# Linformer attention into a maxout FFN on one core: AV made transposed, sums by a ones matmul, q transposed by the DMA crossbar

## The chip, the core and the metric

The kernel runs on one core of a Trainium2 chip. Its engines work side by side, each through its own instructions in order: TensorE (PE, with its weight loads PEld), VectorE (DVE), ScalarE (ACT), GpSimd (POOL) and SyncE (SP). Sixteen DMA engines serve the queues of POOL and SP. The metric is the device time in microseconds; three runs of the kernel before give a median of 466.81 us.

## The reference

Eight batches of eight heads, 1024 positions of 64 elements. K and V are projected along the sequence from 1024 to 64 rows by E and F. Softmax attention over these 64 rows follows. The heads of a position, side by side (512 elements), go through a feed-forward network (FFN) with a maximum of three products.

```python
k_proj = np.einsum('ks,bhsd->bhkd', E, k)
v_proj = np.einsum('ks,bhsd->bhkd', F, v)
scores = scale * np.matmul(q, k_proj.transpose(0, 1, 3, 2))
attn = softmax(scores)                    # over the 64 projected rows
x = np.matmul(attn, v_proj)               # heads side by side: 8192 x 512
h = np.maximum(np.maximum(x @ w1, x @ w2), x @ w3)     # 768 wide
return h @ w_out                          # 8192 x 512, float32
```

## The kernel before

All inputs are cast to bf16 while GpSimd's queue loads them. The kernel is written in a framework whose scheduler fixes, when the program is built, the order of the instructions on each engine and puts in the waits; the order is therefore not just that of the source lines. Tiles come from pools with a number of buffers; an instruction that takes a buffer again waits until its earlier readers are done.

`attention(b)` handles one batch. It loads q, k and v in two halves of 0.5 MB each (L101; `work` has two buffers of each). The K projection `kp_ps` (L108: 16 matmuls of 256 columns, all into partitions 0 to 63) is evicted and transposed, and copied into the block-diagonal `kpT_bd`, two heads to a pair. For each of the four pairs g, a copy brings the pair's q into order (`q_p2`, L135, on VectorE, or on GpSimd for g of 2 and 3 from batch 1 on), eight TensorE transposes (L141) turn it, a copy brings it to SBUF (`qT_sb`, L147), two matmuls of 512 columns make the scores (L154), and ScalarE takes the exponent into `pT_g` (L160). The V projection (L172: 16 matmuls of 256 columns) fills `vp_bd`, which has a column of ones for each head (L189, L190), so that the AV matmul gives the sums as well.

Then for each of eight groups of 128 positions (si), four AV matmuls (L200) have positions on the partitions, VectorE takes the reciprocal of the sums (`zinv`, L209) and multiplies (`x_sb`, L210), four TensorE transposes (L220) turn the result, and a copy puts it into `xT` (L225).

`moe_chunk(b, xT, ch)` is the FFN over 512 positions, two chunks to a batch. For each of six blocks jt, 12 matmuls of 512 columns (L237) fill three banks of PSUM `h_ps`; ScalarE copies the first (`h1s`, L245), VectorE takes the two maxima (`m12`, L247, and `hT`, L248). Then 24 matmuls (L252) make four output tiles, which ScalarE copies to `o_acc` (L259), and SP's queue stores them (L261). The pool `ps_m` of the FFN has three banks, `ps_s` of attention five.

The loop runs attention of batch b ahead of the FFN of batch b-1; the scheduler weaves the two together. The weights (L85, L86) are loaded behind q, k and v of batch 0.

Of the kernel before, what the change touches and what calls it, by code (L numbers as in the profile page):

```python
# [8 lines left out]
FP32 = mybir.dt.float32  # L10
# [6 lines left out]
def kernel(  # L17
# [13 lines left out]
    nc = tc.nc  # L31
# [7 lines left out]
    P = 128  # L39
    SI = 8  # L40
# [10 lines left out]
    xt_pool = ctx.enter_context(tc.tile_pool(name="xt_pool", bufs=B))  # L51
    work = ctx.enter_context(tc.tile_pool(name="work", bufs=2))
    small = ctx.enter_context(tc.tile_pool(name="small", bufs=2))
    moe_sb = ctx.enter_context(tc.tile_pool(name="moe_sb", bufs=2))

    ps_s = ctx.enter_context(tc.tile_pool(name="ps_s", bufs=5, space=bass.MemoryType.PSUM))
    ps_m = ctx.enter_context(tc.tile_pool(name="ps_m", bufs=3, space=bass.MemoryType.PSUM))
# [7 lines left out]

    eT = const.tile([P, SI, KP], BF16, name="eT")
    fT = const.tile([P, SI, KP], BF16, name="fT")
    for src, dst in ((e_sb, eT), (f_sb, fT)):
        tp = ps_s.tile([P, 512], FP32, name="ps_s")
        tpb = tp.bitcast(BF16)  # L70
        src_v = src.rearrange("k (p si) -> k p si", si=SI)
        for si in range(SI):
            nc.tensor.transpose(
                out=tpb[:, si * KP:(si + 1) * KP],
                in_=src_v[:, :, si],
                identity=ident[:KP, :KP],
            )
        nc.any.tensor_copy(out=dst.rearrange("p si k -> p (si k)"), in_=tpb[:, :SI * KP])
# [9 lines left out]
    out_v = out.rearrange("(b p si) m -> b si p m", p=P, si=SI)  # L88

    def attention(b, pending):  # L90
        def drain(n=1):
            for _ in range(min(n, len(pending))):
                moe_chunk(*pending.pop(0))
        k_t = work.tile([P, H, SI, D], BF16, name="k_t")
        v_t = work.tile([P, H, SI, D], BF16, name="v_t")
        q_t = work.tile([P, H, SI, D], BF16, name="q_t")
        for src, dst in ((q[b], q_t), (k[b], k_t), (v[b], v_t)):
            sv = src.rearrange("h (p si) d -> p h si d", si=SI)
            for hh in range(2):
                hs = slice(hh * (H // 2), (hh + 1) * (H // 2))  # L100
                nc.gpsimd.dma_start(out=dst[:, hs], in_=sv[:, hs])  # L101


        kp_ps = ps_s.tile([P, 512], FP32, name="ps_s")
        for hh in range(2):
            hs = slice(hh * (H // 2), (hh + 1) * (H // 2))
            for si in range(SI):
                nc.tensor.matmul(  # L108
                    out=kp_ps[0:KP, hh * (H // 2) * D:(hh + 1) * (H // 2) * D],
                    lhsT=eT[:, si, :],  # L110
                    rhs=k_t[:, hs, si, :],
                    start=(hh == 0 and si == 0),
                    stop=(hh == 1 and si == SI - 1),
                )
        kp_sb = small.tile([P, H, D], BF16, name="kp_sb")
        nc.any.tensor_copy(out=kp_sb[0:KP], in_=kp_ps[0:KP].rearrange("a (h d) -> a h d", d=D))

        kpTs_ps = ps_s.tile([P, 512], FP32, name="ps_s").bitcast(BF16)
        for g in range(NPAIR):
            nc.tensor.transpose(  # L120
                out=kpTs_ps[:, g * KP:(g + 1) * KP],
                in_=kp_sb[0:KP, 2 * g:2 * g + 2, :],
                identity=ident[0:KP, 0:KP],
            )
        kpT_bd = small.tile([P, NPAIR, P], BF16, name="kpT_bd")
        nc.vector.memset(kpT_bd, 0.0)
        kpTs_v = kpTs_ps.rearrange("a (g x) -> a g x", x=KP)[:, :NPAIR, :]
        nc.any.tensor_copy(out=kpT_bd[0:D, :, 0:KP], in_=kpTs_v[0:D])  # L128
        nc.any.tensor_copy(out=kpT_bd[D:2 * D, :, KP:2 * KP], in_=kpTs_v[D:2 * D])

        pT = []
        for g in range(NPAIR):
            q_p2 = small.tile([P, SI, 2 * D], BF16, name="q_p2", bufs=3)
            peng = nc.vector if (b == 0 or g < 2) else nc.gpsimd
            peng.tensor_copy(  # L135
                out=q_p2.rearrange("p si (h d) -> p si h d", h=2),
                in_=q_t[:, 2 * g:2 * g + 2, :, :].rearrange("p h si d -> p si h d"),
            )
            qt_ps = ps_s.tile([P, 512], FP32, name="ps_s").bitcast(BF16)
            for si in range(SI):  # L140
                nc.tensor.transpose(  # L141
                    out=qt_ps[:, si * P:(si + 1) * P],
                    in_=q_p2[:, si, :],
                    identity=ident,
                )
            qT_sb = small.tile([P, SI, P], BF16, name="qT_sb", bufs=2)
            nc.any.tensor_copy(out=qT_sb, in_=qt_ps.rearrange("a (si p) -> a si p", p=P))  # L147

            pT_g = small.tile([P, SI, P], BF16, name="pT_g", bufs=5)
            pT.append(pT_g)  # L150
            for c in range(NCHUNK):
                sc_ps = ps_s.tile([P, 512], FP32, name="ps_s")
                csl = slice(c * SI_PER_CHUNK, (c + 1) * SI_PER_CHUNK)
                nc.tensor.matmul(  # L154
                    out=sc_ps,
                    lhsT=kpT_bd[:, g, :],
                    rhs=qT_sb[:, csl, :],
                    start=True, stop=True,
                )
                nc.scalar.activation(  # L160
                    out=pT_g[:, csl, :],
                    in_=sc_ps,
                    func=AF.Exp,
                    scale=scale,
                )

        vp_e = ps_s.tile([P, 512], FP32, name="ps_s")
        vp_o = ps_s.tile([P, 512], FP32, name="ps_s")
        for par, vt in ((0, vp_e), (1, vp_o)):
            rows = slice(0, KP) if par == 0 else slice(KP, 2 * KP)  # L170
            for si in range(SI):
                nc.tensor.matmul(  # L172
                    out=vt[rows, 0:NPAIR * D],
                    lhsT=fT[:, si, :],
                    rhs=v_t[:, par::2, si, :],
                    start=(si == 0),
                    stop=(si == SI - 1),
                )
        vp_bd = small.tile([P, NPAIR, 2 * (D + 1)], BF16, name="vp_bd")
        nc.vector.memset(vp_bd, 0.0)  # L180
        nc.any.tensor_copy(
            out=vp_bd[0:KP, :, 0:D],
            in_=vp_e[0:KP, 0:NPAIR * D].rearrange("a (g d) -> a g d", d=D),
        )
        nc.any.tensor_copy(  # L185
            out=vp_bd[KP:2 * KP, :, D + 1:2 * D + 1],
            in_=vp_o[KP:2 * KP, 0:NPAIR * D].rearrange("a (g d) -> a g d", d=D),
        )
        nc.vector.memset(vp_bd[0:KP, :, D:D + 1], 1.0)  # L189
        nc.vector.memset(vp_bd[KP:2 * KP, :, 2 * D + 1:2 * D + 2], 1.0)  # L190

        xT = xt_pool.tile([P, NCT, SI, P], BF16, name="xT")
        for si in range(SI):
            x_sb = small.tile([P, H, D], BF16, name="x_sb", bufs=3)
            for u in range(2):
                av_ps = ps_s.tile([P, 512], FP32, name="ps_s")
                av_v = av_ps.rearrange("p (g x) -> p g x", x=256)
                for gg in range(2):
                    g = 2 * u + gg
                    nc.tensor.matmul(  # L200
                        out=av_v[:, gg, 0:2 * D + 2],
                        lhsT=pT[g][:, si, :],
                        rhs=vp_bd[:, g, :],
                        start=(gg == 0),
                        stop=(gg == 1),
                    )
                av_b = av_v[:, :, 0:2 * (D + 1)].rearrange("p g (par y) -> p g par y", par=2)
                zinv = small.tile([P, 2, 2], FP32, name="zinv", bufs=3)
                nc.vector.reciprocal(out=zinv, in_=av_b[:, :, :, D:D + 1])  # L209
                nc.vector.tensor_tensor(  # L210
                    out=x_sb[:, 4 * u:4 * (u + 1), :].rearrange("p (g par) d -> p g par d", par=2),
                    in0=av_b[:, :, :, 0:D],
                    in1=zinv.broadcast_to([P, 2, 2, D]),
                    op=ALU.mult,
                )
            xt_ps = ps_s.tile([P, 512], FP32, name="ps_s").bitcast(BF16)
            xt_v = xt_ps.rearrange("p (ct x) -> p ct x", x=256)
            x_flat = x_sb.rearrange("p h d -> p (h d)")
            for ct in range(NCT):
# [84 lines left out]
```

The softmax here doesn't subtract the row's maximum and nothing guards it: scores larger than these inputs give would overflow.

## Time and profile before

| | |
|---|---|
| median of three runs | 466.81 us (466.43 to 467.7) |
| span of the profiled execution, first to last instruction | 465.2 us, 1.6 us under the median |
| TensorE busy | 431.2 us, 93% |
| VectorE busy | 228.9 us, 49% |
| ScalarE busy | 173.4 us, 37% |
| FFN matmuls on TensorE (L237, L252) | 263.8 and 85.1 us |
| read from and written to HBM | 57.15 and 16.78 MB |

The profile is of one execution. A line of a timeline has the start, the length, the engine, the line of the kernel, the operation, and the tile written and those read; in brackets the engine's idle time before it, and what ended it. The clock (PEclk) is the share of TensorE's full clock that was granted. Matmuls overlap each other, so the time of a run of them is read from its first start to its last end and not from the sum of their lengths. For DMAs, MB are counted at the destination.

### The profile page before, as it was taken

The page shows a single profiled execution, that of the slowest core. Times are in us where ns is not written, and L with a number is a line of the kernel's source. Part 1 is how long each engine was busy: PE and PEld are TensorE (multiplying, and loading weights), DVE is VectorE, ACT ScalarE, POOL GpSimd, SP SyncE. Part 2 cuts the span into 40 slices and gives each one's busy share as a digit, 9 for nine tenths or more (in the row PEclk, how much of TensorE's full clock was granted, in tenths as well). Part 3 has the DMA queues.
Part 4 walks back from the last instruction along what each step waited for, and adds up shares of the span by engine and source line. Part 5 has one row for each costly group of instructions (what it writes and reads, how often), then busy time and mean ns, then how long its engine had stood idle before and what let it go on. Part 6 is the DMA issues. An engine that isn't in the chain of part 4 may idle for free.

```text
span 465.2 us, 6667 instructions
## 1 busy us (share of the span) xinstructions
PE 431.2 (93%) x2623; PEld 226.4 (49%) x2672; DVE 228.9 (49%) x550; ACT 173.4 (37%) x311; POOL 54.7 (12%) x74
## 2 busy tenths in 40 slices
PE   1474999999999999999999999999999999999995
PEld 1343655455544555455544555455544555444442
DVE  2025575527934375426935376425935277334351
ACT  1142555235432543235532553235432453322322
POOL 7212240004000320005000320001000000000000
PEclk9996999999999999999999999999999999999999
DMA  8999999319620691209820592202020200202102
GB/s 118 207 210 206 208 205 207 111 80 171 113 92 0 144 201 20 92 41 189 133 92 1 132 193 39 92 0 92 2 91 0 92 1 0 92 0 92 56 36 90
DMA packets 30208, 45.78 MB, mean 98 GB/s; under 512 B 1121, under 2 KB 28001, under 8 KB 28129
## 3 DMA queue, kind: packets, MB, share of 16 engines
q0 software_dynamic: 27872, 28.58, 38.2%
q1 hardware_dynamic: 2304, 16.78, 8.7%
q8 instruction: 21, 0.34, 0.3%
q14 instruction: 11, 0.08, 0.1%
HBM read 57.15 MB, written 16.78 MB: 159 GB/s over the span
## 4 chain that ended last, share of the span: by engine, by line
PE 89%; DMA 8%; issue 1%; DVE 1%; POOL 1%; ACT 0%; POOLq 0%
PE ps_m L237 53%; PE ps_m L252 18%; DMA q_t<-in_q_dram 5%; PE ps_s L220 3%; PE ps_s L154 3%; PE ps_s L200 3%; PE ps_s L108 3%; PE ps_s L141 3%; DMA k_t<-in_k_dram 2%; PE ps_s L172 2%; PE ps_s L120 0%; DVE qT_sb L147 0%; POOL q_t L101 0%; DVE x_sb L210 0%; DVE zinv L209 0%
## 5 line engine op out<-in xcount | busy, mean ns | idle before, releaser
L237 PE MATMUL ps_m<-xT,w_sb 128*128 128x512 bf16 x1109 | 263.8, 380 | 2.5 <-issue 0.7
L237 PEld LDWEIGHTS <-w_sb 128*128 128x128 bf16 x1152 | 107.5, 98 | 111.8 <-issue 3.3
L245 ACT COPY h1s<-ps_m 128x512 f32<-128x512 f32 x96 | 56.3, 586 | 105.1 <-PE ps_m L237 104.2
L252 PE MATMUL ps_m<-wout_sb,hT 128*128 128x512 bf16 x378 | 85.1, 379 | 0.2
L259 ACT COPY o_acc<-ps_m 128x512 f32<-128x512 f32 x64 | 37.5, 585 | 71.4 <-PE ps_m L252 68.9
L252 PEld LDWEIGHTS <-hT 128*128 128x128 bf16 x384 | 37.3, 98 | 45.2 <-DVE hT L248 3.5
L225 ACT COPY xT<-ps_s 128x512 bf16<-128x512 bf16 x58 | 34.1, 587 | 60.3 <-PE ps_s L220 60.2
L210 DVE TENSOR_TENSOR x_sb<-ps_s,zinv 128x256 bf16<-128x256 f32 x128 | 48.6, 417 | 0.2
L160 ACT ACTIVATE pT_g<-ps_s 128x512 bf16<-128x512 f32 x64 | 34.8, 596 | 19.9 <-PE ps_s L154 19.9
L220 PE MATMUL ps_s<-ident,x_sb 128*128 128x128 bf16 x256 | 35.4, 226 | 5.7 <-DVE x_sb L210 5.6
L220 PEld LDWEIGHTS <-x_sb 128*128 128x128 bf16 x256 | 21.8, 100 | 24.9 <-DVE x_sb L210 13.2
L101 POOL DMA_DIRECT2D k_t<-in_k_dram x16 | 12.0, 753 | 166.1 <-PE ps_s L108 162.5
L200 PE MATMUL ps_s<-vp_bd,pT_g 128*128 128x130 bf16 x256 | 30.4, 227 | 0.5 <-DVE vp_bd L185 0.5
L147 DVE COPY qT_sb<-ps_s 128x1024 bf16<-128x1024 bf16 x31 | 21.4, 691 | 17.5 <-PE ps_s L141 17.5
L108 PE MATMUL ps_s<-k_t,eT 128*64 128x256 bf16 x128 | 17.5, 291 | 10.5 <-DMA k_t<-in_k_dram 10.2
L154 PE MATMUL ps_s<-qT_sb,kpT_bd 128*128 128x512 bf16 x64 | 20.9, 410 | 3.8 <-DVE qT_sb L147 2.4
L128 DVE COPY kpT_bd<-ps_s 64x256 bf16<-64x256 bf16 x6 | 1.7, 283 | 45.2 <-PE ps_s L120 45.2
L209 DVE RECIPROCAL zinv<-ps_s 128x4 f32<-128x4 f32 x128 | 17.8, 170 | 8.3 <-PE ps_s L200 8.1
L108 PEld LDWEIGHTS <-eT 128*64 128x64 bf16 x128 | 14.2, 116 | 13.8 <-issue 12.8
L200 PEld LDWEIGHTS <-pT_g 128*128 128x128 bf16 x256 | 19.5, 101 | 2.6 <-DVE vp_bd L185 2.6
L101 POOL DMA_DIRECT2D v_t<-in_v_dram x16 | 12.0, 762 | 14.2 <-PE ps_s L172 8.2
L172 PE MATMUL ps_s<-v_t,fT 128*64 128x256 bf16 x128 | 13.2, 291 | 0.0
(321 smaller groups left out, 259.0 us busy)
## 6 DMA issues: line engine op xcount, KB each, us to landing
out_dram<-o_acc SPq DMA_DIRECT2D x16, 1024.0 KB, 3.9
q_t<-in_q_dram POOLq DMA_DIRECT2D x16, 512.0 KB, 11.4
k_t<-in_k_dram POOLq DMA_DIRECT2D x16, 512.0 KB, 8.6
v_t<-in_v_dram POOLq DMA_DIRECT2D x16, 512.0 KB, 10.7
w_sb<-in_moe_w_dram POOLq DMA_DIRECT2D x3, 768.0 KB, 22.4
wout_sb<-in_moe_w_out_dram POOLq DMA_DIRECT2D x1, 768.0 KB, 24.9
e_sb<-in_E_dram POOLq DMA_DIRECT2D x1, 128.0 KB, 3.3
f_sb<-in_F_dram POOLq DMA_DIRECT2D x1, 128.0 KB, 3.2
```

What stands on the lines that cost most here:

```text
L101: nc.gpsimd.dma_start(out=dst[:, hs], in_=sv[:, hs])
L108: nc.tensor.matmul(out=kp_ps[0:KP, hh * (H // 2) * D:(hh + 1) * (H // 2) * D], lhsT=eT[:, si, :], rhs=k_t[:, hs, si, :], start=(hh == 0 an ...
L154: nc.tensor.matmul(out=sc_ps, lhsT=kpT_bd[:, g, :], rhs=qT_sb[:, csl, :], start=True, stop=True,)
L160: nc.scalar.activation(out=pT_g[:, csl, :], in_=sc_ps, func=AF.Exp, scale=scale,)
L200: nc.tensor.matmul(out=av_v[:, gg, 0:2 * D + 2], lhsT=pT[g][:, si, :], rhs=vp_bd[:, g, :], start=(gg == 0), stop=(gg == 1),)
L210: nc.vector.tensor_tensor(out=x_sb[:, 4 * u:4 * (u + 1), :].rearrange("p (g par) d -> p g par d", par=2), in0=av_b[:, :, :, 0:D], in1=zinv ...
L220: nc.tensor.transpose(out=xt_v[:, ct, 0:P], in_=x_flat[:, ct * P:(ct + 1) * P], identity=ident,)
L225: nc.any.tensor_copy(out=xT[:, :, si, :], in_=xt_v[:, :, 0:P])
L237: nc.tensor.matmul(out=h_ps[i], lhsT=w_sb[i][:, ct, jt * P:(jt + 1) * P], rhs=rhs_x[:, ct, :, :], start=(ct == 0), stop=(ct == NCT - 1),)
L245: nc.scalar.copy(out=h1s, in_=h_ps[0])
L252: nc.tensor.matmul(out=o_ps, lhsT=hT[:, jt, tt * P:(tt + 1) * P], rhs=wout_sb[:, jt, :], start=(jt == 0), stop=(jt == NJT - 1),)
L259: nc.scalar.copy(out=o_acc[:, tt, :], in_=o_ps)
```

## The change

The attention is written anew, and the order of the two halves of the work with it; the matmuls and evictions of the FFN stay.

- q: `q_p` is filled by four VectorE copies for all pairs of a batch (L117), and one DMA on SP's queue turns the whole of it by the DMA crossbar into `qT` (L122). The TensorE transposes of q and their evictions go.
- K: the projection's two halves of heads go to partitions 0 to 63 and 64 to 127 in turn (L130), so two transposes of 128x128 follow. V: eight matmuls of 512 columns (L155), with F twice beside itself in the weights.
- `kpT_bd` and `vp_bd` are constants with two buffers, set to zero once.
- AV: the weights are the block-diagonal `vp_bd`, the moving data `pT`, so the result has the head's elements on the partitions, as the FFN needs it. The output transposes and their evictions go. A second pair of matmuls with `ones_bd` gives the sums, spread over all 64 partitions of a head (L187).
- The sums are inverted on ScalarE as exp(-ln) in two passes of 128x1024 (L191, L193), and VectorE multiplies straight into `xT` (L194). ScalarE's table for both functions is loaded once at the start.
- `attention` and `ffn` are generators: one step of attention of batch b+1 after each step of the FFN of batch b; attention of batch 0 comes alone. Loads are whole (1 MB for each of q, k, v). Pools: `ps_f` three banks, `ps_a` two of two banks, `ps_p` one.

```diff
+        q_t, k_t, v_t = load(b)
+        q_p = att.tile([P, NPAIR, SI, 2, D], BF16, name="q_p")
+        for g in range(NPAIR):
+            nc.vector.tensor_copy(
+                out=q_p[:, g].rearrange("p si h d -> p h si d"),
+                in_=q_t[:, 2 * g:2 * g + 2, :, :],
+            )
+        qT = att.tile([P, NPAIR * SI, P], BF16, name="qT")
+        nc.sync.dma_start_transpose(
+            out=qT, in_=q_p.rearrange("p g si h d -> p (g si h d)")
+        )
+        yield
...
+        for si in range(SI):
+            for half in range(2):
                 nc.tensor.matmul(
+                    out=kp_ps[half * HALF:(half + 1) * HALF, 0:4 * D],
+                    lhsT=eT2[:, si, half, :],
+                    rhs=k_t[:, 4 * half:4 * half + 4, si, :],
+                    start=(si == 0), stop=(si == SI - 1),
                 )
...
-            qt_ps = ps_s.tile([P, 512], FP32, name="ps_s").bitcast(BF16)
-            for si in range(SI):
-                nc.tensor.transpose(
-                    out=qt_ps[:, si * P:(si + 1) * P],
-                    in_=q_p2[:, si, :],
-                    identity=ident,
-                )
...
+            sc = ps_a.tile([P, 2, 512], FP32, name="ps_a")
+            for c in range(2):
                 nc.tensor.matmul(
+                    out=sc[:, c, :],
                     lhsT=kpT_bd[:, g, :],
+                    rhs=qT[:, g * SI + 4 * c:g * SI + 4 * c + 4, :],
                     start=True, stop=True,
                 )
+            pT = att.tile([P, 2, 512], BF16, name="pT")
+            nc.scalar.activation(out=pT, in_=sc, func=AF.Exp, scale=scale)
+            yield
+            z = ps_a.tile([P, 2, 512], FP32, name="ps_a")
+            av = ps_a.tile([P, 2, 512], FP32, name="ps_a")
+            for dst, w in ((z, ones_bd), (av, vp_bd[:, g, :])):
+                for c in range(2):
                     nc.tensor.matmul(
+                        out=dst[:, c, :], lhsT=w, rhs=pT[:, c, :], start=True, stop=True,
                     )
-                nc.vector.reciprocal(out=zinv, in_=av_b[:, :, :, D:D + 1])
...
-            for ct in range(NCT):
-                nc.tensor.transpose(
-                    out=xt_v[:, ct, 0:P],
-                    in_=x_flat[:, ct * P:(ct + 1) * P],
-                    identity=ident,
-                )
+            zl = att.tile([P, 2, 512], FP32, name="zl")
+            nc.scalar.activation(out=zl, in_=z, func=AF.Ln)
+            zi = att.tile([P, 2, 512], FP32, name="zi")
+            nc.scalar.activation(out=zi, in_=zl, func=AF.Exp, scale=-1.0)
+            nc.vector.tensor_tensor(
+                out=xT[:, g].rearrange("a (c si) p -> a c (si p)", c=2),
+                in0=av, in1=zi, op=ALU.mult,
+            )
+            yield
...
+    for b in range(B):
+        main = ffn(b, box[b])
+        side = attention(b + 1, box) if b + 1 < B else iter(())
+        for _ in main:
+            next(side, None)
+        for _ in side:
+            pass
```

## The prediction

> **What bounds the kernel now.** I read the page's shares and slices first, then the chain that ended last, then the groups by form, and last the start of the run in detail. One batch of attention followed by one batch of the feed-forward network (FFN) is the unit; b is the batch, g the pair of heads.
>
> The page: busy shares, then TensorE, its clock and the DMA engines over 40 slices of 11.6 us.
>
> ```profile
> PE 431.2 (93%) x2623; PEld 226.4 (49%) x2672; DVE 228.9 (49%) x550; ACT 173.4 (37%) x311; POOL 54.7 (12%) x74
> PE   1474999999999999999999999999999999999995
> PEclk9996999999999999999999999999999999999999
> DMA  8999999319620691209820592202020200202102
> ```
>
> TensorE is full from slice 5 on; before that it waits, and the DMA engines are full for the first seven slices. The chain in order of time (start, length, what):
>
> ```profile
> 15.72 24.93 DMA q_t<-in_q_dram
> 101.09 1.86 PE ps_s L108 x16
> 418.34 4.96 PE ps_m L237 x23
> 455.73 4.06 PE ps_m L252 x18
> ```
>
> From the first matmul of batch 2 (101.0 us, L108) to the end of attention (418.3) lie six equal periods of 52.9 us with TensorE on the chain. The last FFN alone runs from 418.34 to 459.79: 192 matmuls in 41.45 us, 215.9 ns each. So attention costs 52.9 - 41.45 = 11.45 us of TensorE per batch, and from the last matmul to the end of the span pass 5.4 us (eviction, output DMA).
>
> Ahead of that, a line each of VectorE's and of TensorE's timeline (start, length, instruction, idle before it and what ended it):
>
> ```profile
> 40.67 0.43 DVE L135 COPY q_p_446<-q_t 128x1024 bf16<-128x1024 bf16 x1 [3.19 <-DMA q_t<-in_q_dram]
> ```
> ```profile
> 41.71 0.40 PE L220 MATMUL ps_s<-ident,x_sb 128*128 128x128 bf16 x2 [3.72 <-DVE x_sb L210]
> ```
>
> This is the pattern my forecast turns on: a q copy for batch 1 stands in VectorE's order ahead of batch 0's x_sb, the copy waits for its load, and TensorE idles 3.72 us. The granted clock then stood at 0.50 from 37.6 to 47.8 us.
>
> DMA queues in two windows, 79 to 81 us and 81.9 to 82.9 us:
>
> ```profile
> q0 software_dynamic: 419, 0.41, 124.7%
> ```
> ```profile
> q0 software_dynamic: 115, 0.11, 65.7%
> q1 hardware_dynamic: 26, 0.21, 51.7%
> ```
>
> Alone, loads move 0.205 MB per us (packets of 1 KB), back to back from 5 to 84 us: a 0.5 MB half lands every 2.54 us. The moment an output DMA runs beside them they fall to 0.11. The load engines have no free room.
>
> **The change, TensorE.** Steady terms first. Removed per batch: 32 q transposes (8 took 0.62 us warm), 32 output transposes (L220), 32 AV matmuls of 130 columns (L200; a pair of both groups runs in 0.23 to 0.43 us). Kept: 8 score matmuls. Added: 8 sum matmuls with ones_bd and 8 AV matmuls, each 512 columns. V's projection becomes 8 of 512 columns instead of 16 of 256. So 32 x 0.216 = 6.92 us, two kp transposes 0.15, and K's projection: 16 of 256 columns took 1.86 us here, all in one half of the partitions; now two halves alternate, 0.93 if a pair overlaps fully. I take 1.4. Attention becomes 8.45 us (8.0 to 8.95), a saving of 3.0 us per batch, some 20 us over seven batches if TensorE never waits.
>
> **Evictions.** ScalarE per batch: three passes of 128x1024 per g. The ScalarE copy of that size took 1.012 us, so 12 x 1.02 = 12.2, plus 20 FFN copies at 0.586, plus two vp copies at 0.37: about 24.7 of a 50 us period. VectorE: 24 maxima at 0.692, four products of 1024 at 1.23 (417 ns at 256, 692 at 512, extended), four copies at 0.42: 24 us. Both fit. Locally: after z and AV, Ln and Exp hold ScalarE until 2.74 us, h1s until 3.37, the product holds VectorE to 4.07 and the next maximum ends at 4.8, where TensorE wants its bank at 4.76. With hand-offs of 0.1 to 0.2 us that is some 0.1 us lost per g, 28 times; I take 2 us, bounds 0 to 14 (half a microsecond each).
>
> **The start, where it is decided.** The loads keep their order and bytes: q, k, v of b=0, weights, then q, k, v of b=1, 2, 3, 4. Batch 1's first q half lands at 40.65 (15.72 + 24.93). To the end of q of b=4 come 19 more halves: 40.65 + 19 x 2.54 = 88.9 us. That each load is now one DMA of 1 MB changes no byte. On GpSimd's queue k and v of b=3 stand ahead of q of b=4 and wait for the projections of batch 1, done by some 57 and 72 us, before the loads ahead of them have drained: nothing.
>
> What moves: in the changed program all four q copies of batch b (L117) go ahead of the crossbar transpose (L122), and VectorE's order has them early. Those of b=1 stand before the last product of b=0; of b=2 before the third maximum of FFN(0); of b=3 before the sixth; of b=4 before the first maximum of FFN(0)'s second chunk. Behind each stand all later maxima, so h_ps is not evicted and TensorE stops after three banks. In the kernel before, b=2 was copied at 56 us just as it landed and later ones far behind, at no cost. Now the second chunk of FFN(0) can't pass until q of b=4 has landed.
>
> By then TensorE has done chunk 0 of FFN(0) and 16 matmuls of chunk 1, and attention(1) up to g=1. That is some 36 us of work available from about 50 us (q of b=1 gates the last product of b=0), so even with its earlier stops it arrives first; this also hides the first transpose's own latency, up to some 30 us. Left after the stop: 1424 FFN matmuls x 0.2159 = 307.4, g=2 and 3 of attention(1) 2.6, six attentions 50.7: 360.7 us.
>
> **The crossbar's price.** Eight transposes of 1 MB, SBUF to SBUF, on SP's queue, on the same 16 engines. The trace has none. Lower bound: an output DMA of 1 MB in 8 KB packets, 8.7% of the span over 16 transfers, 2.5 us each; less is excluded since the engines were full. Upper bound: 32 blocks x 128 partitions are 4096 pieces of 256 B; at a 1 KB packet's price (1024 in 5.08 us) 20 us. I take 5.1, the row with the same megabyte in middling pieces. Transposes of b=0, 1, 2 come before q of b=4 and delay it by 15.2 us. On SP's queue the first output follows them, and transpose 3 follows that output; both start about 97 us and halve the loads for the last 6.4 us, so 6.4 more. q of b=4 lands at 88.9 + 15.2 + 6.4 = 110.5 us.
>
> The Trainium skill, page "VectorE: DVE Perf Modes", section "The three transpose paths", speaks against this change: 1309 ns for a 128x128 block by the crossbar against 390 ns on TensorE, where this trace has 8 TensorE transposes in 0.62 us. As an estimate by that page 32 blocks are 41.9 us, and if all of it were engine time the sum would be near 600. The page "DMA: Bandwidth & Descriptors", section "Latency and other measured facts", gives 261 GB/s for a DMA transpose, by which one is an estimated 4.0 us and the sum 482. No run here shows either yet.
>
> **Sum.** Landing 110.5; four copies, a maximum and hand-offs 2.6; remaining TensorE work 360.7; tail 5.4; evictions 2; clock 3 (the one drop seen lasted 10.2 us at half, partly in the idle time; 0 to 5). Span 484.2 against 465.2. The median of the runs is 1.6 above the span, so 485.8, put as 486.
>
> **Rivals.**
> The crossbar is cheap and TensorE's saving shows: loads are hardly delayed, q of b=4 lands at 90, K's halves overlap (six times 0.45 less), no clock drop or stalls: 90 + 2.6 + 358 + 5.4 + 1.6 = 457.6, faster. For it: TensorE is the chain for 90% of the span and loses 3 us a batch. Against: full engines until 84 us. It decides when q of b=4 lands before 95 us, that is a transpose of under 1 to 2 us.
> The crossbar is dear: at 20 us the landing is 88.9 + 61 + 6.4 = 156 and the time 532; at 10 us 501. For it: small pieces. Against: nothing in the trace but the volume.
> Eviction stalls: half a microsecond at each of 28 places adds 12, 498. Against: 65% busy shares.
> Ln and Exp could reload tables (1.28 us, seen once), but the built order has one load, so this is left out.
>
> **How the numbers follow.** Forecast 0.53 (472 to 495, crossbar 2.5 to 7 us), dear crossbar 0.22, eviction stalls 0.08, cheap crossbar 0.17, of which 0.04 within 0.3% of before. 0.3% (1.4 us) is about what a measurement of this kernel tells from no change. So faster 0.13, same 0.04, slower 0.83. The range leaves out the cheap case and the dear one beyond 20 us: 468 to 530.
>
> **What would show it.** Right: q copies on VectorE waiting for q_t loads between 60 and 115 us, TensorE idle in slices 5 to 9, the clock at 0.5 there, a period near 50 us from batch 2 on, an unchanged tail. Step by step: the landing of q of b=4 (110), the duration of a transpose's packets (5.1), attention per batch (8.45). Wrong: TensorE full from 50 us on, or periods above 53 us, or TensorE waiting for qT in later batches.

## The result and the profile after

The changed kernel takes 484.65 us (median of four, 483.62 to 485.96) against 466.95 for the kernel before on the same chip: a ratio of 1.0371, interval 1.0347 to 1.0396. It is slower by 17.7 us; the forecast was 486. The profiled execution's span is 483.7 us. One execution of a later run, the plain copy, took 2445 us; it is left out as disturbed.

The page of the changed kernel, TensorE, its clock and the DMA engines in 40 slices of 12.1 us:

```profile
PE   0200768087999999999999999999999999999995
PEclk9999999579999999999999999999999999999999
DMA  8999999999969433862467146616202020202012
```

TensorE now idles in slices 3 and 4 (24 to 48 us) and again in slice 8 (85 to 97 us), where the clock has fallen to half. From slice 11 on it is full. The chain of the changed kernel in order of time (start, length, what):

```profile
14.02 35.19 DMA qT<-q_p
...
66.72 48.38 DMA qT<-q_p x2
...
143.14 0.99 PE ps_p L130 x16
...
436.85 15.54 PE ps_f L208 x72
...
473.11 5.19 PE ps_f L225 x24
```

So 35.2 + 48.4 us of the first 115 are crossbar transposes (48.4 is transposes 1 and 2 together); no load of q is on this chain. The q copies of batches 1, 3 and 4 on VectorE, and then the stops on TensorE (start, length, instruction, idle before it and what ended it):

```profile
65.26 1.43 DVE L117 COPY q_p<-q_t 128x1024 bf16<-128x1024 bf16 x4
98.73 1.53 DVE L117 COPY q_p<-q_t 128x1024 bf16<-128x1024 bf16 x4 [14.90 <-DMA qT<-q_p]
115.19 1.43 DVE L117 COPY q_p<-q_t 128x1024 bf16<-128x1024 bf16 x4 [7.42 <-DMA qT<-q_p]
```
```profile
49.25 1.01 PE L174 MATMUL ps_a<-qT,kpT_bd_93 128*128 128x512 bf16 x2 [29.03 <-DMA qT<-q_p]
98.68 1.01 PE L174 MATMUL ps_a<-qT,kpT_bd_94 128*128 128x512 bf16 x2 [15.58 <-DMA qT<-q_p]
117.28 1.89 PE L208 MATMUL ps_f<-xT,w_sb 128*128 128x512 bf16 x8 [2.56 <-DVE m_489 L218]
```

TensorE's two long stops, 29.0 and 15.6 us, are its own waits for `qT` of batches 0 and 1: the scores stand next in its order. On VectorE the copies of batch 3 wait for transpose 1 and those of batch 4 for transpose 2, because `q_p` has two buffers; the FFN's maxima stand behind them. Only the second of these waits shows on TensorE by itself, as the 2.56 us before 117.28. The load of batch 4's q had landed at 103.7 us already.

Why a transpose is so long shows in the queues of the changed kernel, first from 20 to 48 us (beside the loads), then from 126.5 to 133 us (alone): packets, MB, share of the 16 engines. For the second the rate in 40 slices stands first, the time from issue to landing last.

```profile
q0 software_dynamic: 3770, 4.56, 92.7%
q1 hardware_dynamic: 3772, 0.97, 26.2%
```
```profile
GB/s 13 13 13 0 17 183 224 219 216 210 206 216 224 213 221 210 216 221 225 216 222 214 219 214 216 219 216 216 217 219 216 216 214 186 238 27 0 0 0 0
...
q1 hardware_dynamic: 4128, 1.05, 86.0%
...
qT<-q_p SPq DMA_TRANSPOSE x1, 7.3
```

The transpose goes in some 4100 packets of 256 B, and beside the loads one of them passes for each load packet of 1 or 1.5 KB: 3772 against 3770. From issue to landing it takes 7.3 us alone and 35 in company. The loads fall from 0.205 MB per us (the kernel before) to 0.163.

One period of the steady part in the changed kernel (stretch, its length, busy times of TensorE, its weight loads, VectorE, ScalarE, GpSimd, then clock and DMA):

```profile
143.07:192.90 49.83, 49.83 (x245) 22.72 (x246) 23.38 (x36) 23.79 (x34) 1.75 (x2) 1.00 0.60 134
```

It is 49.83 us, all TensorE, against 52.9 before. Six periods bring back 18.4 us of a start that lost about 37: FFN(0) and attention(1) were done at 101.1 us before, at 138.0 now.

### The profile page after: what moved, and what is told of

Read it like the earlier page. It is cut to its first block, busy times and chain, and to the rows that moved or that the text cites. A ratio compares the mean times of both kernels' runs of the same rounds, so it can differ in the third digit from the quotient of the medians.

```text
span 483.7 us, 4961 instructions
## 1 busy us (share of the span) xinstructions
PE 407.9 (84%) x1952; PEld 184.0 (38%) x1952; DVE 191.2 (40%) x291; ACT 192.9 (40%) x273; POOL 26.3 (5%) x36
## 4 chain that ended last, share of the span: by engine, by line
PE 74%; DMA 21%; ACT 2%; DVE 1%; POOL 0%; issue 0%; POOLq 0%; DVEq 0%
PE ps_f L208 47%; DMA qT<-q_p 19%; PE ps_f L225 16%; PE ps_a L187 5%; PE ps_p L155 3%; PE ps_a L174 3%; DMA k_t<-in_k_dram 2%; PE ps_p L130 1%; ACT zl L191 1%; ACT zi L193 1%; ACT pT L181 1%; DVE q_p L117 0%; POOL q_t L107 0%; DVE hT L219 0%; PE ps_p L141 0%
## 5 line engine op out<-in xcount | busy, mean ns | idle before, releaser
L208 PE MATMUL ps_f<-xT,w_sb 128*128 128x512 bf16 x1152 | 263.9, 381 | 4.4 <-DVE m_489 L218 2.6
L225 PE MATMUL ps_f<-wout_sb,hT 128*128 128x512 bf16 x384 | 87.3, 379 | 0.4 <-DVE hT L219 0.4
L216 ACT COPY h1s<-ps_f 128x512 f32<-128x512 f32 x96 | 55.8, 581 | 74.7 <-PE ps_f L208 73.8
L194 DVE TENSOR_TENSOR xT<-ps_a,zi 128x1024 bf16<-128x1024 f32 x32 | 39.2, 1225 | 92.4 <-ACT zi L193 55.1
L181 ACT ACTIVATE pT<-ps_a 128x1024 bf16<-128x1024 f32 x32 | 32.8, 1024 | 90.3 <-PE ps_a L174 90.3
L232 ACT COPY o_acc<-ps_f 128x512 f32<-128x512 f32 x64 | 37.1, 584 | 51.6 <-PE ps_f L225 51.3
L191 ACT ACTIVATE zl<-ps_a 128x1024 f32<-128x1024 f32 x32 | 32.8, 1024 | 45.2 <-PE ps_a L187 45.1
L174 PE MATMUL ps_a<-qT,kpT_bd_93 128*128 128x512 bf16 x32 | 9.9, 393 | 29.6 <-DMA qT<-q_p 29.0
L193 ACT ACTIVATE zi<-zl 128x1024 f32<-128x1024 f32 x32 | 33.8, 1057 | 1.0
L117 DVE COPY q_p<-q_t 128x1024 bf16<-128x1024 bf16 x32 | 12.3, 432 | 32.6 <-DMA qT<-q_p 22.7
L174 PE MATMUL ps_a<-qT,kpT_bd_94 128*128 128x512 bf16 x32 | 9.9, 393 | 15.6 <-DMA qT<-q_p 15.6
L187 PE MATMUL ps_a<-pT,ones_bd 128*128 128x512 bf16 x64 | 19.5, 387 | 4.0 <-ACT pT L181 4.0
L155 PE MATMUL ps_p<-v_t,fT_102 128*128 128x512 bf16 x64 | 16.8, 410 | 0.0
L130 PE MATMUL ps_p<-k_t,eT_101 128*64 128x256 bf16 x128 | 9.9, 294 | 1.9 <-DMA k_t<-in_k_dram 1.9
L187 PEld LDWEIGHTS <-ones_bd 128*128 128x128 bf16 x64 | 6.3, 99 | 12.4 <-issue 5.4
```

The costliest lines, as they stand in the source:

```text
L155: nc.tensor.matmul(out=vp_ps, lhsT=fT2[:, si].rearrange("p x k -> p (x k)"), rhs=v_t[:, :, si, :], start=(si == 0), stop=(si == SI - 1),)
L174: nc.tensor.matmul(out=sc[:, c, :], lhsT=kpT_bd[:, g, :], rhs=qT[:, g * SI + 4 * c:g * SI + 4 * c + 4, :], start=True, stop=True,)
L181: nc.scalar.activation(out=pT, in_=sc, func=AF.Exp, scale=scale)
L187: nc.tensor.matmul(out=dst[:, c, :], lhsT=w, rhs=pT[:, c, :], start=True, stop=True,)
L191: nc.scalar.activation(out=zl, in_=z, func=AF.Ln)
L193: nc.scalar.activation(out=zi, in_=zl, func=AF.Exp, scale=-1.0)
```

## The experiments

Theory A: in the start a transpose is long because its small packets take turns with the loads' packets, and the order on TensorE and VectorE passes that length on to the FFN; in the steady part the change gains 3 us a batch. Theory B: the loads and their extra megabytes are the gate. Theory C: the rest of the rewrite costs it. Each ratio is to the kernel before on the same chip; the landmark for the start is the first K projection of batch 2 (L130 in the changed kernel; some edits shift the line number), at 143.1 us in the changed kernel.

**A plain copy in place of the transpose.**

```diff
-        nc.sync.dma_start_transpose(
-            out=qT, in_=q_p.rearrange("p g si h d -> p (g si h d)")
+        nc.sync.dma_start(
+            out=qT, in_=q_p.rearrange("p g si h d -> p (g si) (h d)")
         )
```

> The crossbar transpose (L122) is replaced by a plain copy of the same megabyte, SBUF to SBUF, on the same queue, with the same waits and the same instruction order; so the scores are made of q that is not transposed. Theory A, the packets: in the changed kernel a transpose goes in 4096 packets of 256 B, one beside each load packet of 1 KB, so it takes 35 us beside the loads (7 us alone) and holds up everything behind it in VectorE's and TensorE's order. A plain copy in large packets takes 3 to 6 us: qT of batch 0 at about 20 us, the FFN of batch 0 from about 48 us, the last stop at the landing of batch 4's q, 88.9 + 4 x 2.5 = 99 us; then 2.1 + 361 + 5.4: a span of 467, time 464 to 472. Rival B, the megabyte: the extra volume and the landing of batch 4's q are the gate, whatever the packets: within 1% of the changed kernel, 480 or more. Rival C, the rest of the rewrite (two extra passes on ScalarE, the new order): also 480 or more.

> The plain copy in place of the transpose once more, for its trace: the scores are made of q that is not transposed. Theory A: a copy lands in 3 to 6 us beside the loads, loads keep over 0.15 MB per us, the copies of batch 4 on VectorE wait for their load and not for a DMA of SP's queue, until about 100 us; period 49.8.

472.1 us, ratio 1.0102 (1.0075 to 1.0128): 0.1 us over what theory A gave, and well under the 480 of both rivals. The trace is of a further execution of the same kernel (473.02 us). From 18 to 22 us, and VectorE's last copies in the start:

```profile
q1 hardware_dynamic: 134, 1.02, 62.7%
q0 software_dynamic: 286, 0.29, 46.8%
```
```profile
99.97 1.43 DVE L117 COPY q_p<-q_t 128x1024 bf16<-128x1024 bf16 x4 [13.89 <-DMA q_t<-in_q_dram]
```

The same megabyte in 8 KB packets passes in some 4 us and the loads give way to it, to 0.07 MB per us. From issue to landing the three copies beside the loads take 9.5, 7.5 and 7.6 us, more than the 3 to 6 expected. Now the copies of batch 4 wait for their load, until 100 us, and L130 of batch 2 comes at 130.2. So the crossbar costs 12.5 us against a plain copy of the same bytes. That the size of its packets does it rests on the count, 3772 against 3770; no run changes the size alone. What is left over the kernel before, 1%, theory A puts down to VectorE's order with the loads; the next four runs bear on that.

**TensorE transposes again, all else as changed.**

```diff
-        nc.sync.dma_start_transpose(...)
+        for g in range(NPAIR):
+            qt_ps = ps_p.tile([P, 512], FP32, name="ps_p").bitcast(BF16)
+            for si in range(SI):
+                nc.tensor.transpose(out=qt_ps[:, si * P:(si + 1) * P], ...)
+            nc.vector.tensor_copy(out=qT[:, g * SI:(g + 1) * SI, :], ...)
```

> q is transposed on TensorE again (32 transposes and four evictions of 128x1024 on VectorE per batch) in one step ahead of the K projection; no crossbar; all else as changed. Theory A: the start is no longer held by transposes, the FFN of batch 0 starts at about 48 us; the period rises from 49.8 by 4 x 0.62 to 52.3 us. 48 + 8 x 41.45 + 7 x 10.9 + 5.4 = 461, with some waits for loads 461 to 468. Rival C (the rewrite's order, not the crossbar, costs the start): 478 or more.

471.84 us, ratio 1.0095 (1.0072 to 1.0118): 3.8 us over the upper end expected. The period is 51.8 us, 2.0 more than with the crossbar, so the crossbar's worth in the steady part is 12 us over six periods. Without it the start still stops for q's loads, as the copies of b=2 and 3 stand ahead of maxima here too (start, length, idle before it and what ended it):

```profile
58.48 0.43 DVE L117 COPY q_p<-q_t 128x1024 bf16<-128x1024 bf16 x1 [4.61 <-DMA q_t<-in_q_dram]
...
73.71 0.43 DVE L117 COPY q_p<-q_t 128x1024 bf16<-128x1024 bf16 x1 [8.04 <-DMA q_t<-in_q_dram]
```

The expected time had left these stops and the clock's drops (three between 45 and 80 us) out. The crossbar therefore is not the whole loss, and theory C's part is this order.

**Four buffers for q_p.**

```diff
-        q_p = att.tile([P, NPAIR, SI, 2, D], BF16, name="q_p")
+        q_p = att.tile([P, NPAIR, SI, 2, D], BF16, name="q_p", bufs=4)
```

> q_p gets four buffers instead of two; nothing else. In the changed kernel the copies of batch 3 wait 14.9 us for transpose 1 to give back its buffer, those of batch 4 wait 7.4 us for transpose 2. Theory A (the transpose's own length is the gate): TensorE needs qT of batch 1 at 98.7 us anyway, so only the second wait's share goes, about 3 us: 480 to 483. Rival D (the buffers are the gate): both waits go, 15 to 20 us, 464 to 470.

491.31 us, ratio 1.051 (1.0486 to 1.0535): slower than either theory said. The copies of batch 3 no longer wait for a buffer (they run at 85.6 us), but TensorE still waits for qT of batch 1:

```profile
99.18 1.01 PE L174 MATMUL ps_a<-qT,kpT_bd 128*128 128x512 bf16 x2 [14.26 <-DMA qT<-q_p]
```

And with buffers free the scheduler put the copies of batches 5 and 6 still further ahead, among the maxima of FFN(0)'s second chunk, where those of batch 6 wait for their load:

```profile
125.10 1.10 DVE L117 COPY q_p<-q_t 128x1024 bf16<-128x1024 bf16 x3 [5.77 <-DMA q_t<-in_q_dram]
```

L130 of batch 2 comes at 148.3, 5.2 us later. A wait for a buffer had also been holding the copies back.

**The copies of batches 1 to 7 on GpSimd.**

```diff
-            nc.vector.tensor_copy(
+            (nc.vector if b == 0 else nc.gpsimd).tensor_copy(
```

> The q copies of batches 1 to 7 go from VectorE to GpSimd (about 1.04 us each there); the crossbar stays. Theory A: transpose 1 can start when its q has landed and been copied, 49.4 + 4.2 = 54 us instead of 66.7, and is done at about 87 instead of 98.7; VectorE holds up no maximum any more, so TensorE stops once, until 87, and then never: 12 us from that, 3 to 4 us from the later stop and the clock: 466 to 472. Rival B (loads or total DMA volume are the gate): within 1% of the changed kernel.

467.69 us, ratio 1.0006 (0.9993 to 1.0019), as theory A had it. The copies wait on GpSimd, up to 31 us, and nothing of the FFN stands behind them:

```profile
POOL q_p L117 <- DMA qT<-q_p: 87.2, 4, 30.7
POOL q_p L117 <- DMA q_t<-in_q_dram: 46.5, 3, 31.0
```

Transpose 1 in the chain (start, length):

```profile
53.25 31.93 DMA qT<-q_p
```

It lands at 85.2 us instead of 98.6, TensorE passes its scores at 85.2 with no stop, and L130 of batch 2 comes at 124.5, 18.6 us earlier. Most of this, 13.5 us, is the earlier start of transpose 1: in the changed kernel the copies of batch 1 stood behind three products of batch 0 on VectorE, until 65.3 us, though their q had landed at 49.4. The stop that the copies of batch 4 made gives 2.6 more. So the place of the q copies in VectorE's order is worth about as much as the whole loss; the crossbar's company with the loads decides how long the rest must wait for them.

**One transpose per pair.**

```diff
+        for g in range(NPAIR):
+            nc.sync.dma_start_transpose(
+                out=qT[:, g * SI:(g + 1) * SI, :],
+                in_=q_p[:, g].rearrange("p si h d -> p (si h d)"),
+            )
```

> One crossbar transpose per pair of heads (256 KB) instead of one per batch; VectorE's order as changed. Theory A (packets share one for one, the length goes by their number): the quarters of batch 0 land at about 23, 32, 41 and 49 us, its attention runs beside them, the copies of batch 1 come at about 53 instead of 65 us, transposes 1 and 2 end some 8 to 12 us earlier: 472 to 478. Rival E (a transpose has a large fixed cost each): no gain or a loss, 484 or more.

484.73 us, ratio 1.0379 (1.0356 to 1.0402): no gain, though the quarters of batch 0 landed at 25.4, 34.6, 42.2 and 49.0 us and transpose 1 was complete at 83.0. Transpose 2 then shared the engines with the loads in its turn, until 110.9, 28 us:

```profile
111.07 1.43 DVE L117 COPY q_p<-q_t 128x1024 bf16<-128x1024 bf16 x4 [17.18 <-DMA qT<-q_p]
```
```profile
113.16 3.57 PE L210 MATMUL ps_f<-xT,w_sb 128*128 128x512 bf16 x8 [9.38 <-DVE m L220]
```

TensorE resumes 4.1 us earlier, but at a granted clock of 0.50 until 117.2 us (eight matmuls 3.57 us against 1.89 in the changed kernel), and the first K projection of batch 2 comes 2.1 us earlier, at 141.0. The time is what rival E had named (484 or more) and not theory A's 472 to 478. But E's cause, a large fixed cost of each transpose, is not seen: the four quarters of batch 0 took 36.2 us together, one transpose 35.2. What counts is where the last transpose of the start ends, and theory A's number had missed that.

**A reciprocal on VectorE for Ln and Exp.**

```diff
-            nc.scalar.activation(out=zl, in_=z, func=AF.Ln)
-            nc.scalar.activation(out=zi, in_=zl, func=AF.Exp, scale=-1.0)
+            nc.vector.reciprocal(out=zi, in_=z)
```

> Ln and Exp on ScalarE are replaced by one reciprocal of 128x1024 on VectorE. Theory A: evictions are hidden in the period (49.8 us against 49.45 of TensorE's own work); at the start each pair is 0.9 us shorter, so the copies of batch 1 and what follows come about 2.5 us earlier: 480 to 485. Rival C (the two passes on ScalarE bind): the period falls too, 475 to 479.

570.19 us, ratio 1.2203 (1.2172 to 1.2235): both expectations fail, for the price of the reciprocal. The group in this kernel, and the two passes in the changed one:

```profile
L191 DVE RECIPROCAL zi<-ps_a 128x1024 f32<-128x1024 f32 x32 | 209.6, 6551 | 40.0 <-PE ps_a L187 39.6
```
```profile
L191 ACT ACTIVATE zl<-ps_a 128x1024 f32<-128x1024 f32 x32 | 32.8, 1024 | 45.2 <-PE ps_a L187 45.1
L193 ACT ACTIVATE zi<-zl 128x1024 f32<-128x1024 f32 x32 | 33.8, 1057 | 1.0
```

One reciprocal takes 6.55 us, exp(-ln) 2.08. With the sums spread over 64 partitions there are 1024 numbers per partition to invert instead of four at a time, and of the two ways run here the table passes are the cheaper by a factor of three. Whether ScalarE binds the period this run can't tell, as VectorE became the bound.

**Both remedies: GpSimd copies, TensorE transposes for batches 0 and 1.**

```diff
-            nc.vector.tensor_copy(
+            (nc.vector if b == 0 else nc.gpsimd).tensor_copy(
...
+        if b < 2:
+            (the four groups of TensorE transposes and copies as above)
+        else:
             nc.sync.dma_start_transpose(...)
```

> Two things together: the q copies of batches 1 to 7 on GpSimd, and q of batches 0 and 1 transposed on TensorE, so that the crossbar runs only from batch 2 on, whose result is not needed before about 105 us. Theory A (in the start a transpose beside the loads takes 35 us and TensorE waits for it; later it is hidden, and the period is 49.8): scores of batch 0 from about 24 us, FFN from 46 to 48, FFN(0) and attention(1) done at about 101 instead of 119 us with the GpSimd copies alone, all else the same: 447 to 454, faster than both kernels. Rival B (the loads and their total volume are the gate): 460 or more.

446.98 us (445.51 to 448.49), ratio 0.957 (0.9545 to 0.9595): 4.3% faster than the kernel before, at the lower edge of what was expected. The start of the kernel with both, 50 to 100 us in the columns of the period shown above:

```profile
50.00:100.00 50.00, 49.96 (x249) 22.90 (x248) 23.36 (x34) 23.89 (x34) 12.29 (x14) 1.00 1.25 199
```

TensorE is full from 50 us while the DMA engines move 199 GB/s, as they do in the changed kernel from 30 to 45 us (198), no drop of the clock shows before the last matmul, and L130 of batch 2 comes at 103.0, 40 us earlier than in the changed kernel. The period stays 49.8. FFN(0) and attention(1) are done at 97.8 us, against 101.1 before. So the loads were not the bound, with crossbar transposes beside them too.

## Why the prediction was right, and where it was not

- **The steady part: right.** Attention at 8.45 us a batch was the term; measured 49.83 - 41.45 = 8.38. K's projection with alternating halves took 0.99 us (taken: 1.4; lower end 0.93), so the alternation overlaps nearly wholly. TensorE's own work then is 8.0, and 0.4 a batch is left, which I put down to evictions (not shown one by one): 2.4 us over six batches for the 2 taken. The tail is 5.4 as before.
- **VectorE's order as the place of the loss: right in part.** The last stop fell where the text had it: resume at 117.28, last matmul at 478.3, 361.0 us between them where 360.7 + 2 stood. But the copies ahead of the maxima cost TensorE only the 2.56 us before it. The long stops, 29.0 and 15.6 us, were TensorE's own waits for qT, and without the wait of b=3 on VectorE (four buffers) the second still lasted 14.3. The costlier place in VectorE's order was another: the copies of b=1, late behind the products.
- **What the copies wait for: wrong.** The step "q of b=4 lands at 110.5 us" named the load; it landed at 103.7. The stop ended with transpose 2, at 115.1. The step that failed is the one before it, "this also hides the first transpose's own latency, up to some 30 us": transposes 0 and 1 took 35.2 and 32 us beside the loads, one after the other, TensorE stood 29.0 and 15.6 us for them, and the buffers of `q_p` chained the copies to them. Of the signs named, the copies' waits for q_t loads between 60 and 115 us did not show. The plain copy shows the forecast's version: there the load does end the stop, at 99.97.
- **The crossbar's price: near as engine time, missing as a wait.** Taken 5.1 us of the engines; alone its packets take 5.6 (86.0% of 6.5 us), beside the loads some 8 (26.2% of 28 us for 0.97 MB). That prices the load's delay well: ahead of q of b=4 came two transposes and the beginning of a third and not three and an output, so it was delayed 14.8 us and not 21.6. But copies and scores wait for the landing, and from issue to landing a transpose takes 7.3 us alone and 32 to 35 beside the loads; for this the sum has no term. The load was 6.8 us earlier than forecast, the gate that took over 4.6 us later, and the 3 us for the clock were not lost. That the total is off by 1.4 us is partly luck.
- **The clock: 3 us taken, none lost.** The drop (85.8 to 102.9 us) fell into the time before the last stop.
- **The rules weighed.** Of the Trainium skill, the 261 GB/s of the page "DMA: Bandwidth & Descriptors", section "Latency and other measured facts", (an estimated 4.0 us; the page gives it for a non-contiguous middle dimension) is not met here: while a transpose alone moves, the trace shows some 216 GB/s, and from issue to landing 1.05 MB in 7.3 us are 144. The 1309 ns a block of its page "VectorE: DVE Perf Modes", section "The three transpose paths", is nearer to what a block costs beside the loads (35.2 / 32 = 1.10 us) than to what it costs alone (0.23). A rule that would have helped stands in the first of these pages, section "Queues, rings and completion order": an engine takes queues in turn, packet by packet. The trace agrees as far as it counts packets, 3772 against 3770 (whether its packets are those of the page no run here shows). By that rule 4096 packets let as many load packets pass, an estimated 4 x 5.08 = 20 us from the load row, and with the 5.6 us of its own packets some 26. Measured from issue to landing are 35.2 and 32 us, and 28 for transpose 2 of the split kernel. The estimate leaves out the 4 us before the first transpose's packets move (two from 14 to 18 us) and that some of its neighbours have 1.5 KB.
- **Rivals.** A cheap crossbar did not come. The dear one came in another form: as latency, not as engine time, and it cost 12.5 us (against the plain copy) and not 46. Eviction stalls of 12 us did not come.

## What to carry to other kernels

Price a DMA that shares engines by its number of packets against its neighbour's, not by its bytes: here small packets beside a saturated load queue stretched it from 7.3 to 35 us, and what waits is its consumer and whatever stands behind that in an engine's order. Look up that order in the built program: a copy that a scheduler has put early, in free buffers, becomes a stop for everything after it when its data come late, and more buffers can make it worse; one that stands late delays the DMA that it feeds. Put such copies on an engine that nothing urgent uses, and keep the slow path for what is not needed soon: in the kernel with both remedies the transposes of batches 2 and 3 still took 32.7 and 28.4 us, and TensorE did not wait.

## What the runs showed of the hardware that I had not expected

- One crossbar transpose of 1 MB, from issue to landing: 7.3 us alone, 35.2 and 32 us for the first two, beside the loads.
- A reciprocal of 128x1024 floats out of PSUM takes 6551 ns on VectorE; the product of the same size, with the same source, 1225.
- Two runs of matmuls with 64 output partitions each, alternating between the halves: 16 of 256 columns in 0.99 us, against 1.86 when all go to one half.
- TensorE's granted clock stood at half for part of the start in every trace but the one with both remedies, from 6.8 us in all (GpSimd copies) to 47 (split transposes), with no plain tie to the stops: in the changed kernel it was at full from 30 to 45 us, a stretch without a matmul, and at half from 85.8 to 102.9 us. Nor does it tell the whole pace: behind the stop of 29 us, at a granted clock of 1.00, the eight matmuls of V's projection took 3.62 us, and 1.89 at 78.6 us.
